# Attention products of one head step on parts of the TensorE array: scores on four 32-column tiles, values on four 32-row tiles

## The chip, the cores and the metric

The kernel runs on one core of a Trainium2 chip. A core has a matrix engine (TensorE, PE in the profile, with its weight loads shown apart as PEld), VectorE (DVE), ScalarE (ACT), GpSimd (POOL) and SyncE (SP), which here issues DMAs. Matrix products read SBUF and write PSUM. The metric is device microseconds of one execution. Six runs of the kernel before gave 1501.7 to 1503.17 us, median 1502.78.

## The reference

The input x has 2048 tokens of 1024 features. It is layer-normalised to xn, and the output is `x + A(xn) + B(xn)`.

A is attention with a small recurrent memory: tokens are cut into 64 segments of 32, each segment is preceded by 8 memory tokens, and 32 heads of 128 features work on these 40 tokens with a causal mask that lets everybody see the memory. The memory rows of a segment's output are the memory of the next segment.

```
for s in range(n_seg):
    h = concatenate([mem, xs])                      # 8 + 32 tokens
    q, k, v = h Wq, h Wk, h Wv                      # 32 heads x 128
    p = softmax(where(mask, q k^T * scale, -1e9))
    o = (p v) Wo
    mem, out_s = o[:8], o[8:]
```

B is a shifted mixer followed by an MLP: `x1 = x + shift(gelu(ln(x) w1)) w2` and `x1 + gelu(ln(x1) w3) w4`, with a hidden width of 3584.

## The kernel before

The program first does B (the mixer with w1 and w2, then the MLP with w3 and w4), and then A. To break the recurrence, A works with an estimate of every segment's memory rows that is computed ahead (tile `MZ`, from mean values), treats the eight memory keys as eight equal entries, and at the end compares the memory that comes out with the estimate. Only if they differ too much would a slow, exact loop at the end of the program run.

A goes through 32 head steps: 4 blocks of 512 tokens (16 segments), and in each block 8 groups of 4 heads. Step i has the block `s.b` and the group `s.hg`. A step has 12 projection chains, counted by c in the loop at lines 897 to 923: c = 0 to 3 are the Q chains of the four heads (`q_chain`, L621), 4 to 7 the K chains (`k_chain`, L637), 8 to 11 the V chains of the four 128-token tiles (`v_chain`, L644). Each is 8 products of 512 columns that accumulate in one PSUM buffer. In the first block each K chain is two runs of 260 columns. The attention products of the step before are hung between the chains: `at(c, f)` calls f after chain c. The order of instructions on each engine is the order of these calls (`manual_schedule`).

For one token tile m of 128 tokens and four heads, `scores` makes per head one product of 128 keys by 132 query columns (four segments of 32 tokens, and one memory column each: W = 33, TW = 132). It lies in the PSUM buffer `psS` (tag A). Of the 128x132 results only the four 32x33 diagonal blocks are wanted, keys of a segment against queries of the same segment. Four exponentials of ScalarE (L671) take these blocks out of `psS` into `ET`. VectorE then transposes in 32x32 blocks (L673), applies the causal mask (L674), sums (L676), takes the reciprocal (L678), normalises (L680) and transposes back (L682). To multiply with the values on the whole array, the probabilities are spread out again into a block-diagonal matrix `BD` of 128x132 per head, with zeros outside the blocks (L686 on VectorE, L688 on POOL for the memory columns). `values` makes one product of 128 keys by 132 columns per head into `psO` (tag B). VectorE adds the estimate `VM` and writes `oX` (L701), and one chain later ScalarE copies the memory columns to `oTs` (L705). POOL also keeps the sums `SSsum` for a check of finiteness and copies the memory scores to `EMs`.

The values of step i come at c = 4, 7, 10 of step i+1 for m = 0, 1, 2 and at c = 1 of step i+2 for m = 3.

PSUM has eight banks: four buffers of one bank with the tag `mm` (`mm_tile`), which all projections and output chains share, and two buffers of two banks, tags A and B (`aux_tile`). A buffer is taken by a new tile when the readers of its last tile are through.

When a block's eight head groups are done, its output projection runs in the second step of the next block (`s.hg == 1`): eight chains of 32 products (`out_chain`, `out_part`, L818), hung at c = 1, each with a load of a piece of `R` (the result of B) that SP issued earlier. For the first block there are also the exact products of the first segment (`first_scores`, `first_soft`, `first_trans`, `first_values`), hung at c = 4, 8, 11 and, a step later, 1. After step 31 a written-out order interleaves the remaining scores and values with the output projection of the last block.

Of the kernel before, what the change touches and what calls it, by code (L numbers as in the profile page):

```python
# [11 lines left out]
DMAX = 1.0e30  # L12

BF16 = mybir.dt.bfloat16
# [7 lines left out]
P = 128  # L22
# [41 lines left out]
def kernel(  # L64
# [69 lines left out]
    def mm_tile(name):  # L134
        return psum.tile([P, 512], F32, tag="mm", bufs=4, name=name)

    def aux_tile(shape, tag, name):
        return psum.tile(shape, F32, tag=tag, bufs=1, name=name)
# [250 lines left out]
    with ExitStack() as p3:  # L389
# [141 lines left out]
        def att_prep():  # L531
            load_xT(0)
            for nm in "qkv":
                need_w(nm, 0)
            need_w("q", 1)
            make_xm(0)
            sm = A["sm"]
            A["BD"] = [sm.tile([P, 4, TW], BF16, name=f"BD{i}") for i in range(3)]
            A["EQ"] = [sm.tile([P, 4, W], F32, name=f"EQ{i}") for i in range(2)]
            for t in A["EQ"]:  # L540
                nc.gpsimd.memset(t[:, :, SEG:W], float(M))
            for nm in ("QZ", "PZ", "VMZ"):
                A[nm] = sm.tile([P, 4, P], BF16, name=nm)
                nc.gpsimd.memset(A[nm][:], 0.0)
            A["VZ"] = sm.tile([P, 512], BF16, name="VZ")
            nc.gpsimd.memset(A["VZ"][:], 0.0)
            A["SS"] = sm.tile([P, 4], F32, name="SSsum")
            nc.gpsimd.memset(A["SS"][:], 0.0)

        for tb in range(4):  # L550
# [29 lines left out]
    specx.close()  # L580

    wpool, xvp, qkv, smp = A["wpool"], A["xvp"], A["qkv"], A["sm"]
    BDs, EQs, SSsum = A["BD"], A["EQ"], A["SS"]
    abig = main.enter_context(tc.tile_pool(name="abig", bufs=1))
    iop = main.enter_context(tc.tile_pool(name="aio", bufs=2))
    oX = abig.tile([P, H, 512], BF16)
# [15 lines left out]
    def new_step(i):  # L602
        s = Step()
        s.i = i
        s.b, s.hg = divmod(i, NHG)
        s.Q = qkv.tile([P, 4, 4 * TW], BF16, tag="Q", bufs=2, name="Q")
        s.K = qkv.tile([P, 4, 512 + M], BF16, tag="K", bufs=2, name="K")
        s.V = qkv.tile([P, 4, 512], BF16, tag="V", bufs=2, name="V")
        if s.hg == 0:
            EMs[s.b] = smp.tile([P, NHG, 4, 4], BF16, tag="EM", bufs=2, name="EM")  # L610
            oTs[s.b] = smp.tile([P, H, 16], BF16, tag="oT", bufs=2, name="oT")
        s.u = [None] * 4
        s.xm = A["m", s.b]
        steps[i] = s
        return s
# [13 lines left out]

    def k_chain(s, hh):  # L630
        w = A["k", s.i]
        n = 2 if s.b == 0 else 1
        c = (512 + M) // 2 if s.b == 0 else 512
        for h2 in range(n):
            ps = mm_tile("psK")
            for k in range(KT):
                nc.tensor.matmul(ps[:, 0:c], w[:, k, hh * P:(hh + 1) * P], s.xm[:, k, h2 * c:(h2 + 1) * c], start=(k == 0), stop=(k == KT - 1))  # L637
            nc.scalar.copy(s.K[:, hh, h2 * c:(h2 + 1) * c], ps[:, 0:c])  # L638

    def v_chain(s, m):  # L640
        w = A["v", s.i]
        ps = mm_tile("psV")
        for k in range(KT):
            nc.tensor.matmul(ps[:], s.xm[:, k, m * P:(m + 1) * P], w[:, k, :], start=(k == 0), stop=(k == KT - 1))  # L644
        nc.scalar.copy(s.V[:, m, :], ps[:])  # L645
# [11 lines left out]
    def mem_cols(s):  # L657
        nc.gpsimd.tensor_copy(s.Q[:].rearrange("p h (s i) -> p h s i", i=W)[:, :, :, SEG], QM[:, hsl(s.hg), 7 + 16 * s.b:23 + 16 * s.b])

    un = [0]  # L660

    def scores(s, m):
        n = un[0]
        un[0] += 1
        ps = aux_tile([P, 4, 256], "A", "psS")
        for hh in range(4):
            nc.tensor.matmul(ps[:, hh, 0:TW], s.K[:, hh, m * P:(m + 1) * P], s.Q[:, hh, m * TW:(m + 1) * TW], start=True, stop=True)  # L667
        ET = smp.tile([P, 4, W], F32, tag="ET", bufs=2, name="ET")
        for j in range(4):
            q = slice(SEG * j, SEG * (j + 1))  # L670
            nc.scalar.activation(ET[q, :, :], ps[q, :, W * j:W * (j + 1)], ACTF.Exp, scale=SCALE)  # L671
        EQ = EQs[n % 2]
        nc.vector.transpose(EQ[:, :, 0:SEG], ET[:, :, 0:SEG])  # L673
        nc.vector.tensor_tensor(EQ[:, :, 0:SEG], EQ[:, :, 0:SEG], causal[:].unsqueeze(1).to_broadcast((P, 4, SEG)), op=ALU.mult)  # L674
        ss = smp.tile([P, 4], F32, tag="ss", bufs=2, name="ss")
        nc.vector.tensor_reduce(ss[:], EQ[:], axis=AX.X, op=ALU.add)  # L676
        rs = smp.tile([P, 4], F32, tag="rs", bufs=2, name="rs")
        nc.vector.reciprocal(rs[:], ss[:])  # L678
        Pn = smp.tile([P, 4, SEG], BF16, tag="Pn", bufs=2, name="Pn")
        nc.vector.tensor_tensor(Pn[:], EQ[:, :, 0:SEG], rs[:].unsqueeze(2).to_broadcast((P, 4, SEG)), op=ALU.mult)  # L680
        PT = smp.tile([P, 4, SEG], BF16, tag="PT", bufs=2, name="PT")
        nc.vector.transpose(PT[:], Pn[:])  # L682
        BD = BDs[n % 3]
        B4 = BD[:].rearrange("p h (j i) -> p h j i", i=W)
        so = segone[:].unsqueeze(1).to_broadcast((P, 4, 4))
        nc.vector.tensor_tensor(B4[:, :, :, 0:SEG], PT[:].unsqueeze(2).to_broadcast((P, 4, 4, SEG)),  # L686
                                so.unsqueeze(3).to_broadcast((P, 4, 4, SEG)), op=ALU.mult)
        nc.gpsimd.tensor_tensor(B4[:, :, :, SEG], ET[:, :, SEG:W].to_broadcast((P, 4, 4)), so, op=ALU.mult)  # L688
        nc.gpsimd.tensor_tensor(SSsum[:], SSsum[:], ss[:], op=ALU.add)
        nc.gpsimd.tensor_copy(EMs[s.b][:, s.hg, :, m:m + 1], ET[:, :, SEG:W])  # L690
        s.u[m] = BD

    def values(s, m):
        BD = s.u[m]
        ps = aux_tile([P, 4, 256], "B", "psO")
        for hh in range(4):
            nc.tensor.matmul(ps[:, hh, 0:TW], s.V[:, m, hh * P:(hh + 1) * P], BD[:, hh, :], start=True, stop=True)  # L697
        p4 = ps[:, :, 0:TW].rearrange("p h (j i) -> p h j i", i=W)
        j0 = 1 if (s.b == 0 and m == 0) else 0
        z = 7 + 16 * s.b + 4 * m  # L700
        nc.vector.tensor_tensor(  # L701
            oX[:, hsl(s.hg), m * P:(m + 1) * P].rearrange("p h (j i) -> p h j i", i=SEG)[:, :, j0:4, :],
            p4[:, :, j0:4, 0:SEG],
            VM[:, hsl(s.hg), z + j0:z + 4].unsqueeze(3).to_broadcast((P, 4, 4 - j0, SEG)), op=ALU.add)
        return lambda: nc.scalar.copy(oTs[s.b][:, hsl(s.hg), 4 * m:4 * m + 4], p4[:, :, :, SEG])  # L705

    QZ, PZ, VMZ, VZ = A["QZ"], A["PZ"], A["VMZ"], A["VZ"]

# [83 lines left out]
        total(d, 0, M)  # L792

    def finite():
        cnt = smp.tile([P, 5], F32, tag="cnt", name="cnt")
        nc.vector.tensor_scalar(cnt[:, 0:4], SSsum[:], DMAX, None, op0=ALU.is_le)
        nc.vector.tensor_reduce(cnt[:, 4:5], cnt[:, 0:4], axis=AX.X, op=ALU.add)
        nc.vector.tensor_scalar(chk[:, 2 * NV:2 * NV + 1], cnt[:, 4:5], -1.0, 4.0, op0=ALU.mult, op1=ALU.add)

    Rts = {}  # L800

# [47 lines left out]
    for i in range(NS):  # L849
# [7 lines left out]
        def at(c, f, *a):  # L857
            hooks.setdefault(c, []).append((f, a))

        def at_values(c, u, m):  # L860
            later = []
            at(c, lambda: later.append(values(u, m)))
            at(c + 1, lambda: later.pop()())

        if pp is not None:
            at_values(1, pp, 3)
        if p is not None:
            at(0, scores, p, 0)
            for m in range(3):
                at(3 * m + 3, scores, p, m + 1)  # L870
                at_values(3 * m + 4, p, m)
        if 4 < s.hg and s.b + 1 < NB:
            for k in range(3 * s.hg - 15, min(3 * s.hg - 12, KT)):
                at(2 + 4 * (k % 3), make_xm, s.b + 1, (k,))
# [5 lines left out]
            at(1, first_values, pp)  # L880
        if s.hg == 1 and s.b > 0:
            for c in range(8):
                at(1, out_chain, s.b - 1, c)
        if s.hg == 2 and s.b > 0:
            at(2, norm_sums, s.b - 1)
            for j in range(4):
# [37 lines left out]
        if last:  # L924
            b = s.b
            load_Rt(b, 0)
            load_Rt(b, 1)
            hp = H - 4
            scores(s, 0)
            out_part(b, 0, 0, hp)  # L930
            values(p, 3)()
            scores(s, 1)
            out_part(b, 1, 0, hp)
            values(s, 0)()
            scores(s, 2)
            out_part(b, 2, 0, hp)
            values(s, 1)()
            scores(s, 3)
            out_part(b, 0, hp, H)
            out_part(b, 1, hp, H)  # L940
            out_part(b, 3, 0, hp)
            values(s, 2)()
            out_part(b, 2, hp, H)
            out_part(b, 3, hp, H)
            values(s, 3)()
            norm_sums(b)
            for j in range(4):
                norm_recip(b, j)
            norm_apply(b)
            norm_add(b)  # L950
            compare(b)
            finite()
            out_chain(b, 4)
            out_chain(b, 5)
            out_chain(b, 6)
            verdict()
            out_part(b, 7, 0, H, 2)
# [129 lines left out]
```

## Time and profile before

| | |
|---|---|
| median of six runs | 1502.78 us |
| the profiled execution | 1502.8 us |
| its span, first to last instruction | 1501.0 us |
| granted TensorE clock | 1.000 |
| instructions | 23719 |
| matrix products / weight loads | 9330 / 9456 records |
| score products (L667) | 512 of 128x132, 221 ns each |
| value products (L697) | 512 of 128x132, 221 ns each |
| exponentials (L671) | 512 of 32x132, 271 ns each |
| VectorE spreading into `BD` (L686) | 128, 703 ns each |
| VectorE adding into `oX` (L701) | 120 of 128x512, 683 ns each, and 8 shorter |

A line of a group names the source line, the engine, the operation, the tiles (written, then read), and for TensorE the part of the array that is used as rows*columns ahead of the shape of the moving operand; then the count, the busy time in us, the mean duration of one in ns, and the idle time of the engine just before. Products are pipelined: the next one starts long before the last has left the array, so a duration of 221 ns is not the time that one more product costs. Their busy time is the union of the durations. The timeline has the start in us, the time until the last one of the row ends, the engine, line and tiles, and the count of instructions merged in the row.

### The profile page before, as it was taken

The page shows a single profiled execution, that of the slowest core. Times are in us where ns is not written, and L with a number is a line of the kernel's source. Part 1 is how long each engine was busy: PE and PEld are TensorE (multiplying, and loading weights), DVE is VectorE, ACT ScalarE, POOL GpSimd, SP SyncE. Part 2 cuts the span into 40 slices and gives each one's busy share as a digit, 9 for nine tenths or more (in the row PEclk, how much of TensorE's full clock was granted, in tenths as well). Part 3 has the DMA queues.
Part 4 walks back from the last instruction along what each step waited for, and adds up shares of the span by engine and source line. Part 5 has one row for each costly group of instructions (what it writes and reads, how often), then busy time and mean ns, then how long its engine had stood idle before and what let it go on. Part 6 is the DMA issues. An engine that isn't in the chain of part 4 may idle for free.

```text
span 1501.0 us, 23719 instructions
## 1 busy us (share of the span) xinstructions
PE 1486.1 (99%) x9330; PEld 784.9 (52%) x9456; DVE 666.5 (44%) x1561; ACT 467.5 (31%) x1247; POOL 257.2 (17%) x707
## 2 busy tenths in 40 slices
PE   9999999999999999999999999999999999999998
PEld 7844444444444466666644544444544544444544
DVE  8283010010110226666622777731676650576654
ACT  5633202103012035454501444420434430244420
POOL 6152131211110202121210111110111110111110
PEclk9999999999999999999999999999999999999999
DMA  8599753553121545474522454431455441344302
GB/s 216 138 283 214 264 189 99 184 174 133 63 92 40 199 136 188 143 223 141 183 71 64 139 166 141 154 102 50 140 153 156 141 133 58 105 138 140 117 0 72
DMA packets 189172, 208.11 MB, mean 139 GB/s; under 512 B 50168, under 2 KB 157832, under 8 KB 189056
## 3 DMA queue, kind: packets, MB, share of 16 engines
q1 hardware_dynamic: 180768, 178.82, 39.6%
q0 software_dynamic: 8288, 27.72, 5.3%
q8 instruction: 76, 1.25, 0.4%
q14 instruction: 40, 0.33, 0.1%
HBM read 170.07 MB, written 25.17 MB: 130 GB/s over the span
## 4 chain that ended last, share of the span: by engine, by line
PE 98%; DMA 1%; issue 0%; SPq 0%; DVE 0%
PE psK L637 15%; PE psP L818 15%; PE psQ L621 15%; PE psV L644 15%; PE ps L555 13%; PE ps L573 13%; PE ps L366 4%; PE ps L265 3%; PE psO L697 2%; PE psS L667 2%; PE psM L653 1%; DMA w_sb<-in_B_w_dram 1%; PE psvb L425 1%; PE psG L446 1%; PE ps L294 0%
## 5 line engine op out<-in xcount | busy, mean ns | idle before, releaser
L818 PE MATMUL psP<-wo_sb,oX 128*128 128x512 bf16 (+1 forms) x1036 | 221.7, 372 | 1.1
L671 ACT ACTIVATE ET<-psS 32x132 f32<-32x132 f32 x512 | 139.0, 271 | 203.7 <-PE psS L667 198.1
L573 PE MATMUL ps<-w,hT_all 128*128 128x512 bf16 x874 | 193.7, 379 | 1.2
L637 PE MATMUL psK<-xT,w 128*128 128x512 bf16 x747 | 176.3, 379 | 1.1
L621 PE MATMUL psQ<-xT,w 128*128 128x512 bf16 x750 | 175.8, 379 | 1.1
L644 PE MATMUL psV<-w,xT 128*128 128x512 bf16 x745 | 175.0, 379 | 1.0
L818 PEld LDWEIGHTS <-oX 128*128 128x128 bf16 x1056 | 102.9, 98 | 115.7
L637 PEld LDWEIGHTS <-w 128*128 128x128 bf16 x1280 | 121.3, 98 | 80.1
L556 ACT ACTIVATE hT_all<-ps 128x512 bf16<-128x512 f32 x112 | 66.8, 597 | 283.5 <-PE ps L555 283.5
L621 PEld LDWEIGHTS <-w 128*128 128x128 bf16 x1024 | 96.8, 98 | 104.1
L573 PEld LDWEIGHTS <-hT_all 128*128 128x128 bf16 x896 | 87.1, 98 | 103.8
L688 POOL TENSOR_TENSOR BD<-ET,c_segone_sb 128x16 bf16<-128x16 f32 x128 | 33.7, 263 | 491.5 <-ACT ET L671 491.5
L628 DVE TENSOR_TENSOR Q<-psQ,QM 128x512 bf16<-128x512 f32 (+1 forms) x128 | 85.6, 679 | 60.9 <-ACT Q L627 39.8
L644 PEld LDWEIGHTS <-xT 128*128 128x128 bf16 x768 | 72.1, 98 | 73.5
L673 DVE STREAM_TRANSPOSE EQ<-ET 128x128 f32<-128x128 f32 x128 | 39.8, 311 | 157.0 <-ACT ET L671 156.8
L645 ACT CAST V<-psV 128x512 bf16<-128x512 f32 x128 | 75.0, 586 | 110.1 <-PE psV L644 100.1
L638 ACT CAST K<-psK 128x512 bf16<-128x512 f32 (+1 forms) x160 | 80.4, 502 | 90.8 <-PE psK L637 89.0
L555 PE MATMUL ps<-xn3T,w3a 128*128 128x512 bf16 x448 | 97.7, 379 | 0.0
L555 PE MATMUL ps<-xn3T,w3b 128*128 128x512 bf16 x448 | 97.7, 379 | 0.0
L824 DVE TENSOR_TENSOR ot<-psP,Rt 128x512 bf16<-128x512 f32 (+1 forms) x33 | 22.2, 675 | 157.3 <-PE psP L818 157.3
L686 DVE TENSOR_TENSOR BD<-PT,c_segone_sb 128x512 bf16<-128x512 bf16 x128 | 90.0, 703 | 4.5
L701 DVE TENSOR_TENSOR oX<-psO,VM 128x512 bf16<-128x512 f32 (+1 forms) x128 | 86.3, 674 | 7.8 <-PE psO L697 7.8
(157 smaller groups left out, 1499.8 us busy)
## 6 DMA issues: line engine op xcount, KB each, us to landing
w<-in_A_Wq_dram SPq DMA_DIRECT2D x32, 1024.0 KB, 5.4
w<-in_A_Wk_dram SPq DMA_DIRECT2D x32, 1024.0 KB, 5.4
w<-in_A_Wv_dram SPq DMA_DIRECT2D x32, 1024.0 KB, 5.4
R_scratch<-x POOLq DMA_DIRECT2D x16, 512.0 KB, 7.2
R<-R_scratch SPq DMA_DIRECT2D x16, 512.0 KB, 7.1
chunk<-in_A_Wv_dram SPq DMA_DIRECT2D x8, 1024.0 KB, 5.4
R_scratch<-R POOLq DMA_DIRECT2D x16, 512.0 KB, 4.1
chunk<-in_A_Wo_dram SPq DMA_DIRECT2D x8, 1024.0 KB, 5.8
```

Source lines behind the costliest of these rows:

```text
L555: nc.tensor.matmul(ps[:], w3[:, k, (f % FH) * P:(f % FH + 1) * P], xn3Ts[tb][:, :, k, :], start=(k == 0), stop=(k == KT - 1))
L573: nc.tensor.matmul(ps[:], h3T[:, f, j * P:(j + 1) * P], w4t[f // 4][:, f % 4, ch * 512:(ch + 1) * 512], start=(f == 0), stop=(f == FT - 1))
L621: nc.tensor.matmul(ps[:], w[:, k, hh * P:(hh + 1) * P], s.xm[:, k, 0:512], start=(k == 0), stop=(k == KT - 1))
L628: nc.vector.tensor_tensor(q3[:, j0:16, 0:SEG], p3_[:, j0:16, :], QM[:, 4 * s.hg + hh, z + j0:z + 16].unsqueeze(2).to_broadcast((P, 16 - j0 ...
L637: nc.tensor.matmul(ps[:, 0:c], w[:, k, hh * P:(hh + 1) * P], s.xm[:, k, h2 * c:(h2 + 1) * c], start=(k == 0), stop=(k == KT - 1))
L638: nc.scalar.copy(s.K[:, hh, h2 * c:(h2 + 1) * c], ps[:, 0:c])
L644: nc.tensor.matmul(ps[:], s.xm[:, k, m * P:(m + 1) * P], w[:, k, :], start=(k == 0), stop=(k == KT - 1))
L645: nc.scalar.copy(s.V[:, m, :], ps[:])
L671: nc.scalar.activation(ET[q, :, :], ps[q, :, W * j:W * (j + 1)], ACTF.Exp, scale=SCALE)
L686: nc.vector.tensor_tensor(B4[:, :, :, 0:SEG], PT[:].unsqueeze(2).to_broadcast((P, 4, 4, SEG)), so.unsqueeze(3).to_broadcast((P, 4, 4, SEG) ...
L701: nc.vector.tensor_tensor(oX[:, hsl(s.hg), m * P:(m + 1) * P].rearrange("p h (j i) -> p h j i", i=SEG)[:, :, j0:4, :], p4[:, :, j0:4, 0:SE ...
L818: nc.tensor.matmul(ps[:, 0:w], oX[:, h, m * P:(m + 1) * P], wo_sb[:, h, cc], start=(h == 0), stop=(h == H - 1))
```

## The change

Scores and values of a step are each done for all four heads and all four token tiles at once, 16 items (m, head), on parts of the array.

`scores` makes for each item and each segment j a product of that segment's 32 keys by its own 33 query columns. The 32 keys are the weights; the output goes to the 32 PSUM partitions of segment j, so that the four segments use four 32-column tiles of the array. 64 products fill two `mm` buffers, and two exponentials read them whole.

`soft` runs the same VectorE sequence as before, once for the 16 items (512 columns instead of four times 128). There is no block-diagonal spreading, except for the last item.

`values` makes for 15 of the items and each segment j a product with the segment's 32 rows of V and of the probabilities: 60 products on four 32-row tiles, into four banks (one for each j) of the tags A and B. Fifteen items of 33 columns are what fits into a bank; the sixteenth is one ordinary product of 128 rows by 132 columns with a `BD` of its own, into an `mm` buffer `psE`. VectorE adds into `oX` with nine instructions, and `mem_values` copies the memory columns with seven ScalarE instructions.

All of it is hung at c = 7: the scores of step i-1, then the values of step i-2, then the softmax of step i-1; `mem_values` follows at c = 10. The output chains of a finished block move from c = 1 to c = 9. K and V tiles are taken at their first chain instead of at the step's start. The end of the program is put into a new order.

```diff
-    def scores(s, m):
-        ps = aux_tile([P, 4, 256], "A", "psS")
-        for hh in range(4):
-            nc.tensor.matmul(ps[:, hh, 0:TW], s.K[:, hh, m * P:(m + 1) * P], s.Q[:, hh, m * TW:(m + 1) * TW], start=True, stop=True)
-        for j in range(4):
-            nc.scalar.activation(ET[q, :, :], ps[q, :, W * j:W * (j + 1)], ACTF.Exp, scale=SCALE)
...
+    def scores(s):
+        s.ps = [mm_tile("psS") for _ in range(2)]
+        s.ET = smp.tile([P, 16, W], F32, tag="ET", name="ET")
+        for g in range(2):
+            for it in range(8):
+                m, hh = divmod(8 * g + it, 4)
+                for j in range(4):
+                    k0 = m * P + SEG * j
+                    nc.tensor.matmul(s.ps[g][SEG * j:SEG * (j + 1), it * W:(it + 1) * W], s.K[:, hh, k0:k0 + SEG],
+                                     s.Q[:, hh, (4 * m + j) * W:(4 * m + j + 1) * W], start=True, stop=True)
+            nc.scalar.activation(s.ET[:, 8 * g:8 * g + 8, :], s.ps[g][:, 0:8 * W].rearrange("p (t i) -> p t i", i=W), ACTF.Exp, scale=SCALE)
+
+    def soft(s):
+        nc.vector.transpose(EQ[:, :, 0:SEG], ET[:, :, 0:SEG])
...
+        nc.vector.transpose(s.PT[:, :, 0:SEG], Pn[:])
+        nc.gpsimd.tensor_copy(s.PT[:, :, SEG:W], ET[:, :, SEG:W])
...
+    def values(s):
+        s.O = [aux_tile([P, 2, 512], t, "psO") for t in "AB"]
+        s.E = mm_tile("psE")
+        for it in range(15):
+            for j in range(4):
+                m, hh = divmod(it, 4)
+                q = slice(SEG * j, SEG * (j + 1))
+                nc.tensor.matmul(s.O[j // 2][:, j % 2, it * W:(it + 1) * W], s.V[q, m, hh * P:(hh + 1) * P], s.PT[q, it, 0:W], start=True, stop=True)
+        nc.tensor.matmul(s.E[:, 0:TW], s.V[:, 3, 3 * P:4 * P], s.BD[:], start=True, stop=True)
...
-        if pp is not None:
-            at_values(1, pp, 3)
         if p is not None:
-            at(0, scores, p, 0)
-            for m in range(3):
-                at(3 * m + 3, scores, p, m + 1)
-                at_values(3 * m + 4, p, m)
+            at(7, scores, p)
+        if pp is not None:
+            at(7, values, pp)
+            at(10, mem_values, pp)
+        if p is not None:
+            at(7, soft, p)
...
-                at(1, out_chain, s.b - 1, c)
+                at(9, out_chain, s.b - 1, c)
...
-            scores(s, 0)
+            scores(s)
+            values(p)
+            soft(s)
             out_part(b, 0, 0, hp)
-            values(p, 3)()
-            scores(s, 1)
+            mem_values(p)
             out_part(b, 1, 0, hp)
-            values(s, 0)()
-            scores(s, 2)
+            values(s)
             out_part(b, 2, 0, hp)
-            values(s, 1)()
-            scores(s, 3)
+            mem_values(s)
             out_part(b, 0, hp, H)
             out_part(b, 1, hp, H)
-            out_part(b, 3, 0, hp)
-            values(s, 2)()
             out_part(b, 2, hp, H)
-            out_part(b, 3, hp, H)
-            values(s, 3)()
+            out_chain(b, 3)
             norm_sums(b)
```

More of the change, by code (lines that the diff above doesn't have):

```diff
@@ L537, in att_prep @@
             sm = A["sm"]
[L538 to L541, printed above, removed]
+            A["EQ"] = sm.tile([P, 16, W], F32, name="EQ")
+            nc.gpsimd.memset(A["EQ"][:, :, SEG:W], float(M))
             for nm in ("QZ", "PZ", "VMZ"):
@@ L546, in att_prep @@
             nc.gpsimd.memset(A["VZ"][:], 0.0)
-            A["SS"] = sm.tile([P, 4], F32, name="SSsum")
+            A["SS"] = sm.tile([P, 16], F32, name="SSsum")
             nc.gpsimd.memset(A["SS"][:], 0.0)
@@ L582 @@
     wpool, xvp, qkv, smp = A["wpool"], A["xvp"], A["qkv"], A["sm"]
-    BDs, EQs, SSsum = A["BD"], A["EQ"], A["SS"]
+    EQ, SSsum = A["EQ"], A["SS"]
     abig = main.enter_context(tc.tile_pool(name="abig", bufs=1))
@@ L606, in new_step @@
         s.Q = qkv.tile([P, 4, 4 * TW], BF16, tag="Q", bufs=2, name="Q")
-        s.K = qkv.tile([P, 4, 512 + M], BF16, tag="K", bufs=2, name="K")
-        s.V = qkv.tile([P, 4, 512], BF16, tag="V", bufs=2, name="V")
         if s.hg == 0:
@@ L611, in new_step @@
             oTs[s.b] = smp.tile([P, H, 16], BF16, tag="oT", bufs=2, name="oT")
-        s.u = [None] * 4
         s.xm = A["m", s.b]
@@ L631, in k_chain @@
         w = A["k", s.i]
+        if hh == 0:
+            s.K = qkv.tile([P, 4, 512 + M], BF16, tag="K", bufs=2, name="K")
         n = 2 if s.b == 0 else 1
@@ L641, in v_chain @@
         w = A["v", s.i]
+        if m == 0:
+            s.V = qkv.tile([P, 4, 512], BF16, tag="V", bufs=2, name="V")
         ps = mm_tile("psV")
@@ L658, in mem_cols @@
         nc.gpsimd.tensor_copy(s.Q[:].rearrange("p h (s i) -> p h s i", i=W)[:, :, :, SEG], QM[:, hsl(s.hg), 7 + 16 * s.b:23 + 16 * s.b])
-    un = [0]
-    def scores(s, m):
-        n = un[0]
-        un[0] += 1
-        ps = aux_tile([P, 4, 256], "A", "psS")
-        for hh in range(4):
-            nc.tensor.matmul(ps[:, hh, 0:TW], s.K[:, hh, m * P:(m + 1) * P], s.Q[:, hh, m * TW:(m + 1) * TW], start=True, stop=True)
-        ET = smp.tile([P, 4, W], F32, tag="ET", bufs=2, name="ET")
-        for j in range(4):
-            q = slice(SEG * j, SEG * (j + 1))
-            nc.scalar.activation(ET[q, :, :], ps[q, :, W * j:W * (j + 1)], ACTF.Exp, scale=SCALE)
[L672 to L705, printed above, removed]
+    def scores(s):
[9 more added lines that the diff above has]
+            nc.scalar.activation(s.ET[:, 8 * g:8 * g + 8, :], s.ps[g][:, 0:8 * W].rearrange("p (t i) -> p t i", i=W), ACTF.Exp, scale=SCALE)
@@ new lines, in soft @@
+    def soft(s):
+        ET = s.ET
+        nc.vector.transpose(EQ[:, :, 0:SEG], ET[:, :, 0:SEG])
+        nc.vector.tensor_tensor(EQ[:, :, 0:SEG], EQ[:, :, 0:SEG], causal[:].unsqueeze(1).to_broadcast((P, 16, SEG)), op=ALU.mult)
+        ss = smp.tile([P, 16], F32, tag="ss", name="ss")
+        nc.vector.tensor_reduce(ss[:], EQ[:], axis=AX.X, op=ALU.add)
+        rs = smp.tile([P, 16], F32, tag="rs", name="rs")
+        nc.vector.reciprocal(rs[:], ss[:])
+        Pn = smp.tile([P, 16, SEG], BF16, tag="Pn", name="Pn")
+        nc.vector.tensor_tensor(Pn[:], EQ[:, :, 0:SEG], rs[:].unsqueeze(2).to_broadcast((P, 16, SEG)), op=ALU.mult)
+        s.PT = smp.tile([P, 16, W + 1], BF16, tag="PT", name="PT")
+        nc.vector.transpose(s.PT[:, :, 0:SEG], Pn[:])
+        nc.gpsimd.tensor_copy(s.PT[:, :, SEG:W], ET[:, :, SEG:W])
+        s.BD = smp.tile([P, TW], BF16, tag="BD", name="BD")
+        nc.gpsimd.tensor_tensor(s.BD[:].rearrange("p (j i) -> p j i", i=W), s.PT[:, 15, 0:W].unsqueeze(1).to_broadcast((P, 4, W)),
+                                segone[:].unsqueeze(2).to_broadcast((P, 4, W)), op=ALU.mult)
+        nc.gpsimd.tensor_tensor(SSsum[:], SSsum[:], ss[:], op=ALU.add)
+        nc.gpsimd.tensor_copy(EMs[s.b][:, s.hg, :, :].rearrange("p h m -> p m h"), ET[:].rearrange("p (m h) i -> p m h i", h=4)[:, :, :, SEG])
@@ new lines, in values @@
+    def values(s):
[7 more added lines that the diff above has]
+        nc.tensor.matmul(s.E[:, 0:TW], s.V[:, 3, 3 * P:4 * P], s.BD[:], start=True, stop=True)
+        z = 7 + 16 * s.b
+        h0 = 4 * s.hg
+        e3 = s.E[:, 0:TW].rearrange("p (j i) -> p j i", i=W)
+        nc.vector.tensor_tensor(oX[:, h0 + 3, 3 * P:4 * P].rearrange("p (j i) -> p j i", i=SEG), e3[:, :, 0:SEG],
+                                VM[:, h0 + 3, z + 12:z + 16].unsqueeze(2).to_broadcast((P, 4, SEG)), op=ALU.add)
+        for j in range(4):
+            o4 = s.O[j // 2][:, j % 2, 0:15 * W].rearrange("p (t i) -> p t i", i=W)
+            for m0, m1, hn in ((1 if s.b == 0 and j == 0 else 0, 3, 4), (3, 4, 3)):
+                n = (m1 - m0) * hn
+                nc.vector.tensor_tensor(
+                    oX[:, h0:h0 + hn, :].rearrange("p h (m c) -> p m h c", c=P)[:, m0:m1, :, SEG * j:SEG * (j + 1)],
+                    o4[:, 4 * m0:4 * m0 + n, 0:SEG].rearrange("p (m h) i -> p m h i", h=hn),
+                    VM[:, h0:h0 + hn, z:z + 16].rearrange("p h (m j) -> p m h j", j=4)[:, m0:m1, :, j].unsqueeze(3).to_broadcast((P, m1 - m0, hn, SEG)), op=ALU.add)
@@ new lines, in mem_values @@
+    def mem_values(s):
+        h0 = 4 * s.hg
+        oT = oTs[s.b]
+        e3 = s.E[:, 0:TW].rearrange("p (j i) -> p j i", i=W)
+        nc.scalar.copy(oT[:, h0 + 3, 12:16], e3[:, :, SEG])
+        for r in range(2):
+            o4 = s.O[r][:, :, 0:15 * W].rearrange("p j (t i) -> p j t i", i=W)[:, :, :, SEG]
+            for j in range(2):
+                nc.scalar.copy(oT[:, h0:h0 + 4, :].rearrange("p h (m j) -> p m h j", j=4)[:, 0:3, :, 2 * r + j], o4[:, j, 0:12].rearrange("p (m h) -> p m h", h=4))
+            nc.scalar.copy(oT[:, h0:h0 + 3, 12 + 2 * r:14 + 2 * r].rearrange("p h j -> p j h"), o4[:, :, 12:15])
@@ L794, in finite @@
     def finite():
[L795 to L798, printed above, removed]
+        cnt = smp.tile([P, 17], F32, tag="cnt", name="cnt")
+        nc.vector.tensor_scalar(cnt[:, 0:16], SSsum[:], DMAX, None, op0=ALU.is_le)
+        nc.vector.tensor_reduce(cnt[:, 16:17], cnt[:, 0:16], axis=AX.X, op=ALU.add)
+        nc.vector.tensor_scalar(chk[:, 2 * NV:2 * NV + 1], cnt[:, 16:17], -1.0, 16.0, op0=ALU.mult, op1=ALU.add)
     Rts = {}
@@ L858, in at @@
             hooks.setdefault(c, []).append((f, a))
[L860 to L863, printed above, removed]
+        if p is not None:
+            at(7, scores, p)
         if pp is not None:
-            at_values(1, pp, 3)
+            at(7, values, pp)
+            at(10, mem_values, pp)
         if p is not None:
-            at(0, scores, p, 0)
-            for m in range(3):
-                at(3 * m + 3, scores, p, m + 1)
-                at_values(3 * m + 4, p, m)
+            at(7, soft, p)
         if 4 < s.hg and s.b + 1 < NB:
```

## The prediction

> **What bounds the kernel now.** I read five views: busy time by engine, the chain that ended last, the groups by form, and the timeline at two places.
>
> ```profile
> PE 1486.1 (99%) x9330; PEld 784.9 (52%) x9456; DVE 666.5 (44%) x1561; ACT 467.5 (31%) x1247; POOL 257.2 (17%) x707
> ...
> PE 98%; DMA 1%; issue 0%; SPq 0%; DVE 0%
> ```
>
> TensorE is the chain from end to end; no other engine sets the time. So the change is worth what it does to TensorE's time. VectorE's 44% and ScalarE's 31% matter only if they make TensorE wait. In the chain in order of time, one head step looks like this:
>
> ```profile
> 1204.01 0.23 PE psS L667 x4
> ...
> 1205.97 0.23 PE psO L697 x4
> 1206.20 3.45 PE psQ L621 x16
> ```
>
> Four score products take 0.23 us, then the projections go on at once. The groups, each shape apart (count | busy us, mean ns of one | idle before):
>
> ```profile
> L697 PE MATMUL psO<-BD,V 128*128 128x132 bf16 x512 | 50.9, 221 | 0.1
> L667 PE MATMUL psS<-Q,K 128*128 128x132 bf16 x512 | 50.4, 221 | 0.0
> L425 PE MATMUL psvb<-xb,chunk 128*128 128x63 bf16 x256 | 9.0, 193 | 0.0
> L260 PE MATMUL psX<-c_segone_sb,x 128*128 128x4 bf16 x128 | 4.3, 164 | 0.0
> L725 PE MATMUL psZ<-KZ,QZ 128*128 128x40 bf16 x32 | 2.1, 180 | 0.0
> ```
>
> Matmuls overlap, so the pace (start to start of two load-and-multiply pairs) has to be worked out: a run of n lasts one duration plus n-1 paces. psS: 128 runs of 4 in 50.4 us are 394 ns each, (394-221)/3 = 57.6 ns for 132 columns. psvb: 8 runs of 32, (1125-193)/31 = 30 ns for 63 columns. psZ: 8 runs of 4, about 27 ns for 40. psX: 8 runs of 16, (537-164)/15 = 25 ns for 4 columns. Below some 50 columns a pair costs about 25 ns however short it is. Two places already use a part of the array, 8 rows (L400) and one column (L835, L837):
>
> ```profile
> 125.50 1.03 PE L366 MATMUL ps<-w_sb,hT_all 128*128 128x512 bf16 x4
> 126.46 0.35 PE L400 MATMUL ps<-c_eye_sb,m 8*128 8x9 bf16 x8
> 126.74 1.04 PE L555 MATMUL ps<-xn3T,w3a 128*128 128x512 bf16 x4
> ```
>
> ```profile
> 1488.21 0.81 PE L818 MATMUL psP<-wo_sb,oX 128*128 128x512 bf16 x3
> 1488.95 0.08 PEld L835 LDWEIGHTS <-c_qones_sb 128*1 128x1 bf16 x1 [0.42 <-issue]
> 1488.95 0.22 PE L835 MATMUL psC<-chk,c_qones_sb 128*1 128x141 bf16 x1
> 1488.95 0.21 PEld L837 LDWEIGHTS <-c_qones_sb 128*1 128x1 bf16 x3
> 1489.01 0.35 PE L837 MATMUL psC<-chk,c_qones_sb 128*1 128x141 bf16 x3
> ...
> 1489.29 0.77 PEld L818 LDWEIGHTS <-oX 128*128 128x128 bf16 x8
> ```
>
> The 8-row run: (350-162)/7 = 27 ns a pair, the floor again. Switching costs: the last 512-column product before L400 starts at 125.50+1.03-0.38 = 126.15, so the next was due 0.216 us later at 126.37; it starts at 126.46, 0.09 us late. Leaving is 0.07 us late. Around the one-column run both are 0.09 us late. So a change of shape costs about 93 ns.
>
> **The change, part by part.** Own time of the profiled execution: 1502.8 us, span 1501.0 with 1.8 around it, at the median of the runs (1502.78).
>
> Removed from TensorE: per head step 16 score and 16 value pairs of 132 columns, eight runs of 0.231 us (4 x 57.6), 1.85 us; 32 steps make 59.2 us. Even free products could save no more.
>
> Added: per step 64 score pairs (32 columns of weights, 33 streamed) and 60 value pairs (32 rows, 33 streamed), 124 pairs, plus one ordinary pair of 57.6 ns for the sixteenth item. No row shows 33 columns on four different tiles. From below: if the tiles fully overlap, four pairs share one 25 ns slot, 6.25 ns. From above: psvb's pace is 30 ns and the one-column pairs' is 61 ns for 141 columns; a weight load that no longer hides under so short a product could add some 15 ns, so 40 ns. I take 25 ns: 33 columns lie between psX's 4 and psZ's 40, and the only row with a narrow row tile, L400, stands there too. 32 x 124 x 25 ns = 99.2 us; the ordinary pair 1.8 us.
>
> Shape changes: full to column tiles, to row tiles, to full, three a step: 32 x 3 x 93 ns = 8.9 us, where before there were none (a product after a run of psS starts 58 ns on, a plain pace). Bounds: nothing if the loads run ahead, 12 us if each were 0.12.
>
> PSUM: the mm ring has four buffers. psE holds one from c=7 until its ScalarE copy at c=10. In steps with the first segment's work (7 of them hold psE as well), psVZ and psZ take two more after the first value projection, so the next projection waits for the 586 ns V copy with only 4 x 56 + 4 x 25 = 320 ns of products as cover: 0.3 us, 2.1 us in all (0 to 4). Elsewhere a projection of 1.73 us covers the copy in the three buffers left; so it does for the eight output chains now at c=9.
>
> VectorE: four softmax and expansion rounds of 3.05 us a step (311+292+291+178+292+311+703+674 ns) become one of about 3.7 and nine adds of about 3.5 us (384-element adds 544 ns in L701's short form): 12.2 to 7.2 us. ScalarE: sixteen exponentials of 271 ns become two of about 0.39 (L267's 256 columns), four copies of 173 ns become seven. POOL's small work shrinks. None is gained, because TensorE's "idle before" psS and psO is 0.0 and 0.1 us. It does not hurt either: work bunched at c=7 ends about 10.6 us later, the first Q projection that needs VectorE ends at 3.4 + 5 x 1.73 = 12.0 us, and behind it three more buffers are free. If this cover went, each us late would be a us a step, 32 us. The output chains need the adds only at heads 28 to 31, 6 us in. At the end, values wait for softmax (11 us) behind 12 us of output products. No DMA is added; SP's and POOL's queues keep their loads. Moving the output chains from c=1 to c=9 puts their R loads in SP's queue behind the k and v weight loads (5.4 us each); the third chain is the first to need one, 13.8 us later.
>
> Sum: -59.2 + 99.2 + 1.8 + 8.9 + 2.1 = +52.8 us, to 1555.6.
>
> A rule on it: the Trainium skill, "TensorEngine Tiling (Array Packing)", Instruction Overhead, gives each matmul about 60 cycles whatever its free size below 60, and warns against taking the tiling factor from a dimension already small. This change takes it from 132 columns to 33; by that rule each pair stays at the 25 ns measured. Against it, "TensorE: Matmul & The Clock Gate", Part 3, has tiles of one pack start some 4 ns apart; an estimate of 8 ns for load and product gives 31.7 us instead of 99.2, and 1488. No run shown here has such a pack.
>
> **The rivals.**
>
> *The tiles overlap* (other side). Four neighbours write separate partitions or banks, and use different weights. For it: at 1488.95 two weight loads and a product start within one hundredth of a microsecond, so the front end can start instructions far quicker than every 25 ns. Against: no two products in the trace start closer than 25 ns. At 6.25 ns: 24.8 + 12.8 - 59.2 = -21.6, 1481. It decides below (59.2-12.8)/(32 x 124) = 11.7 ns a pair; between 6 and 11 lies 1481 to 1500. Instruction fetch sets a limit near that: 76 packets of the instruction queue took 0.4% of 16 x 1501 us, 1.3 us for 16 KB; 248 short instructions are nearly one packet in 1 us.
>
> *Half overlap*: only one product, or loads limiting at 12 to 20 ns. Score pairs at 6.25 and value pairs at 25: 32 x (64 x 6.25 + 60 x 25) = 60.8, +14.4, 1517.
>
> *Dearer pairs*: the 32-column loads don't hide. At 33 ns +84.6 (1587), at 40 +112 (1615). For it: load and product now last about equally long. Against: in the one-column run the next load starts under the running product.
>
> **How the numbers follow.** Serial at the floor, 22 to 30 ns: 0.42, 1544 to 1575, my forecast 1555.6. Half overlap: 0.16, 1503 to 1544. Full overlap: 0.30, 1480 to 1501. Dearer: 0.12, above 1575. Faster is the full overlap without its edge, 0.28; same (within 0.2%, 3 us, about what a measurement tells from no change) 0.04 at 11 to 12.5 ns; slower 0.68. The range is 1480 to 1592: it leaves out the dearest pairs (0.08) and a little below.
>
> **What would show it.** psS and psO runs: 64 and 60 pairs at 25 ns, so 1.6 and 1.5 us of chain each step, then 1.73 us projections untouched; starts 0.09 us late at three places a step; VectorE busy near 500 us and TensorE still at 98% or more. Wrong if neighbouring starts of different tiles stand closer than 12 ns, if weight loads rather than products set the pace, or if TensorE waits for PSUM in most steps.

## The result, and the profile after

The changed kernel takes 1498.77 us (median of 18 runs, 1497.81 to 1500.97) against 1502.49 us before: ratio 0.9976, 95% interval 0.9969 to 0.9982. It is 3.7 us faster, where 52.8 us slower was forecast. The profiled execution has a span of 1497.4 us, 3.6 less than before.

Busy time by engine and the head of the chain that ended last, after:

```profile
PE 1472.1 (98%) x12314; PEld 760.2 (51%) x12432; DVE 500.7 (33%) x1017; ACT 347.1 (23%) x895; POOL 196.8 (13%) x450
...
PE 95%; DVE 3%; issue 1%; DMA 1%; SPq 0%; ACT 0%; POOL 0%; DVEq 0%; POOLq 0%; ACTq 0%
```

TensorE's busy time fell by 14.0 us although it runs some 3000 products more. The span fell only by 3.6 us: TensorE is now idle for 25.3 us of it, before for 14.9, and VectorE has a place of 3% in the chain, where it had none. So there are two questions: why did the products become cheaper, and where did the rest of the gain go?

The groups by form, after (count | busy us, mean ns of one | idle before):

```profile
L667 PE MATMUL psS<-Q,K 128*32 128x33 bf16 x2048 | 21.7, 182 | 0.0
L697 PE MATMUL psO<-PT,V 32*128 32x33 bf16 x1920 | 20.0, 177 | 0.0
```

and a step of a later block in the chain in order of time:

```profile
1172.73 0.61 PE psS L667 x64
1173.34 0.56 PE psO L697 x60
1173.90 0.16 PE psE L698
```

All attention products of a step, their changes of shape included, take 1.33 us. Before it was eight runs of 0.23, 1.85 us. Of the 0.61 us, some 0.10 is the change of shape behind it, so 64 pairs take 0.51 us, 8 ns a pair; the value pairs come to 7.5 ns. In the trace the starts lie in groups of four, 3 to 4 ns apart, and each group begins some 25 ns after the start of the one before it. So the four tiles do work at the same time, and the 25 ns that the trace of before showed for every short pair is what one tile needs, not what the engine needs. This regular picture holds for the first 32 pairs after a change of shape (6.3 ns a pair); the later ones follow evenly at 8.3 ns.

The length of a step is the time from its first Q product to that of the next step. Before, a step of block 0 and one of block 3 in the chain in order of time:

```profile
654.34 0.21 PE psQ L621
...
679.75 0.22 PE psQ L621
...
1202.29 1.73 PE psQ L621 x8
...
1224.86 1.73 PE psQ L621 x8
```

and after:

```profile
658.31 0.22 PE psQ L616
...
684.78 0.22 PE psQ L616
...
1203.02 4.10 PE psQ L616 x19
...
1225.07 4.10 PE psQ L616 x19
```

A steady step of blocks 1 to 3 takes 22.05 us after and 22.57 to 22.58 before: 0.525 us gained. Times 32 this is 16.8 us. But in block 0 such a step takes 26.46 us after and 25.41 before: 1.05 us lost. What TensorE waited for, the four longest in total (us, times, longest):

```profile
PE psV L643 <- DVE eZ L744: 6.0, 7, 0.9
PE psV L643 <- ACT V L644: 2.5, 7, 0.4
PE psE L698 <- issue: 1.9, 1, 1.9
PE psT L252 <- DVE xn L229: 1.8, 2, 1.0
```

Before, only its waits in the first 15 us stood there. Seven steps of block 0 have two waits each. The timeline of one shows how they come about (start, time to the end of the last one, in brackets the idle time before):

```profile
673.99 2.47 DVE L708 TENSOR_TENSOR oX<-psO,VM 128x256 bf16<-128x256 f32 x8
...
675.53 0.26 PE L742 MATMUL psZ<-KZ,QZ 128*128 128x40 bf16 x4
...
676.14 3.61 PE L643 MATMUL psV<-w,xm 128*128 128x512 bf16 x16 [0.36 <-ACT V L644]
...
679.66 0.71 DVE L682 STREAM_TRANSPOSE PT<-Pn 128x512 bf16<-128x512 bf16 x1
680.29 0.27 DVE L744 SCALAR_TENSOR_TENSOR eZ<-psZ,c_mask_sb 40x160 f32<-40x160 f32 x1
...
680.62 1.89 PE L643 MATMUL psV<-w,xm 128*128 128x512 bf16 x8 [0.86 <-DVE eZ L744]
```

psZ, the first segment's scores, is complete at 675.8, but VectorE still has the adds of the values and then the whole softmax of 16 items in its queue. It reads psZ at 680.29. Until then psZ holds one of the four `mm` buffers, psE holds another, and the V chains wait: once for the V copy and once for psZ. Measured start to start the two cost 0.51 and 1.07 us, 1.58 a step, 11.0 us in seven steps. The third wait, 1.9 us once in step 3, has no releaser in the profile.

In sum: -16.8 + 11.0 + 1.9 = -3.9 us; the measured spans differ by -3.6.

### The profile page after: what moved, and what is told of

It reads as the page before. It is cut to its first block, busy times and chain, and to the rows that moved or that the text cites. A ratio compares the mean times of both kernels' runs of the same rounds, so it can differ in the third digit from the quotient of the medians.

```text
span 1497.4 us, 28216 instructions
## 1 busy us (share of the span) xinstructions
PE 1472.1 (98%) x12314; PEld 760.2 (51%) x12432; DVE 500.7 (33%) x1017; ACT 347.1 (23%) x895; POOL 196.8 (13%) x450
## 4 chain that ended last, share of the span: by engine, by line
PE 95%; DVE 3%; issue 1%; DMA 1%; SPq 0%; ACT 0%; POOL 0%; DVEq 0%; POOLq 0%; ACTq 0%
PE psK L634 15%; PE psP L835 15%; PE psQ L616 15%; PE ps L553 13%; PE ps L571 13%; PE psV L643 12%; PE ps L366 4%; PE ps L265 3%; PE psS L667 1%; PE psO L697 1%; PE psM L652 1%; DVE oX L708 1%; DMA w_sb<-in_B_w_dram 1%; PE psvb L425 1%; PE psG L446 1%
## 5 line engine op out<-in xcount | busy, mean ns | idle before, releaser
L634 PEld LDWEIGHTS <-w 128*128 128x128 bf16 x1280 | 125.1, 98 | 99.1
L643 PE MATMUL psV<-w,xT 128*128 128x512 bf16 x744 | 169.2, 379 | 2.5 <-DVE eZ L744 0.9
L616 PE MATMUL psQ<-xT,w 128*128 128x512 bf16 x744 | 169.1, 379 | 1.3
L634 PE MATMUL psK<-xT,w 128*128 128x512 bf16 x763 | 169.4, 379 | 0.3
L616 PEld LDWEIGHTS <-w 128*128 128x128 bf16 x1024 | 98.8, 98 | 115.9
L702 DVE TENSOR_TENSOR oX<-psE,VM 128x128 bf16<-128x128 f32 x32 | 9.3, 292 | 217.9 <-PE psE L698 217.9
L708 DVE TENSOR_TENSOR oX<-psO,VM 128x96 bf16<-128x96 f32 (+2 forms) x256 | 82.1, 393 | 0.0
L553 PEld LDWEIGHTS <-w3b 128*128 128x128 bf16 x448 | 43.5, 98 | 52.0
L553 PEld LDWEIGHTS <-w3a 128*128 128x128 bf16 x448 | 43.5, 98 | 51.7
L481 DVE TENSOR_SCALAR xt<-xt,lnst 128x1024 bf16<-128x1024 bf16 x16 | 8.7, 546 | 180.6 <-POOL R L480 180.6
```

What stands on the lines that cost most here:

```text
L553: nc.tensor.matmul(ps[:], w3[:, k, (f % FH) * P:(f % FH + 1) * P], xn3Ts[tb][:, :, k, :], start=(k == 0), stop=(k == KT - 1))
L616: nc.tensor.matmul(ps[:], w[:, k, hh * P:(hh + 1) * P], s.xm[:, k, 0:512], start=(k == 0), stop=(k == KT - 1))
L708: nc.vector.tensor_tensor(oX[:, h0:h0 + hn, :].rearrange("p h (m c) -> p m h c", c=P)[:, m0:m1, :, SEG * j:SEG * (j + 1)], o4[:, 4 * m0:4 ...
```

## The experiments

Every ratio is to the kernel before, run on the same chip; in parentheses stands its 95% interval. The edits are against the changed kernel, and dots mark lines left out.

**Pairs of one tile in a row.** Is it the change of tile that makes the pairs cheap?

```diff
-            for it in range(8):
+            for it, j in [(it, j) for j in range(4) for it in range(8)]:
...
-        for it in range(15):
-            for j in range(4):
+        for it, j in [(it, j) for j in range(4) for it in range(15)]:
```

> Same products as the changed kernel, but all items of segment 0 first, then segment 1 and so on, so that 8 score pairs and 15 value pairs in a row go to the same tile. Theory (pairs on different tiles overlap, a tile by itself takes a new pair only every 25 ns): the pace of psS and psO goes from 8 ns to about 25 ns, 124 x 17 ns = 2.1 us a step, 32 steps +67 us, about 1566 us. Rival (a narrow pair is cheap in itself, whatever tile the one before it was on): pace still 8 ns, about 1499 us.

1539.69 us, ratio 1.0248 (1.0232 to 1.0264), 41 us above the changed kernel. The same products in the chain of a steady step:

```profile
1174.19 1.15 PE psS L666 x64
1175.33 1.36 PE psO L695 x60
```

Less the 0.10 us for the change of shape behind each, this is 16 and 21 ns a pair. Within a tile the trace has start after start 25 or 26 ns apart; around the seam from one tile to the next the spacings alternate (3, 23, 2, 23 ns), as they would if pairs of both ran at once, and the mean stays below 25. Direction and floor are as the theory has it, the rise of 67 us was too high because it left out these seams. A narrow pair is not cheap in itself.

**Two tiles alternating.**

```diff
-            for it in range(8):
+            for it, j in [(it, j) for h in (0, 2) for it in range(8) for j in (h, h + 1)]:
...
-        for it in range(15):
-            for j in range(4):
+        for it, j in [(it, j) for h in (0, 2) for it in range(15) for j in (h, h + 1)]:
```

> Same products, alternating between segments 0 and 1 and then between 2 and 3. Theory (each tile takes a pair every 25 ns, and 8 ns is the pace at which pairs are handed out): two tiles give 12.5 ns a pair, 124 x 4.5 ns x 32 = +18 us, about 1517 us. Rival (any change of tile is enough, the pace is that of the handing out): 8 ns, about 1499 us.

1508.27 us, ratio 1.0042 (1.0029 to 1.0055), 9.5 us above the changed kernel. Score and value pairs take 9.7 and 11.3 ns in the mean; in the regular stretches two starts lie 2 to 5 ns apart and the next two 25 ns on, 12.5 ns a pair. Again the seam between the halves saves something. With one, two and four tiles the pace in the regular stretches is 25, 12.5 and 6.3 ns: a tile takes one pair every 25 ns. In these kernels each tile also has its own place in PSUM (32 partitions for the scores, a bank for the values); no run tells a limit of the tile from one of that place.

**More changes of shape.** Scores and values in halves, interleaved.

```diff
-            at(7, scores, p)
+            at(7, scores, p, (0,))
...
-            at(7, values, pp)
+            at(7, values, pp, range(8))
...
+            at(7, scores, p, (1,))
...
+            at(7, values, pp, range(8, 15))
```

> The changed kernel with scores and values cut in halves and interleaved (scores 0, values 0, scores 1, values 1): five changes of the array's shape a step instead of three, the same pairs. Theory (a change of shape costs about 0.1 us each time, as L400 and the one-column run showed): 2 x 0.1 us x 31 steps = +6 us, about 1505 us. Rival (the changes run under the pairs): no difference, 1499 us.

1500.29 us, ratio 0.9988 (0.9978 to 0.9997): 1.5 us above the changed kernel, not 6. A steady step:

```profile
1173.06 0.31 PE psS L668 x32
1173.37 0.30 PE psO L699 x32
1173.68 0.31 PE psS L668 x32
1173.99 0.28 PE psO L699 x28
1174.27 0.16 PE psE L702
```

1.36 us instead of 1.33. Each change does cost its time (start to start 110 ns from scores to values and 102 back, of which some 6 are the pairs' own pace), but the pairs now run at 6.6 ns in the mean instead of 8.0 and 7.5, because each run ends before the slower stretch begins. Both theories were half right. Why the first 32 pairs run at 6.3 ns and the later ones at 8.3 was not tried; the supply of instructions is one candidate.

**The first segment's work ahead of the bundle.**

```diff
-            at(4, first_scores, p)
-            at(8, first_soft, p)
+            at(2, first_scores, p)
+            at(5, first_soft, p)
```

> The changed kernel with the first segment's exact products earlier in the step: first_scores after chain 2 instead of 4, first_soft after chain 5 instead of 8, so ahead of the bundle at chain 7. Theory (the gain is given back in the first block, where psVZ and psZ come right behind the bundle, find three PSUM buffers, and VectorE reads psZ only after 7 us of queued work): 7 steps x 1.58 us = 11 us gone, about 1488 us. Rival (the first block has to wait for that work wherever it is put): the stalls move to the K chains and the time stays near 1499 us.

1486.76 us, ratio 0.9898 (0.9883 to 0.9914), 12.0 us below the changed kernel. All that TensorE still waited for:

```profile
PE psW L197 <- DVE fill L176: 1.5, 1, 1.5
PE psO L697 <- issue: 1.4, 1, 1.4
PE psT L252 <- DVE xn L229: 1.2, 2, 0.8
PE ps L280 <- ACT xn2T L255: 0.2, 1, 0.2
```

Both waits of the V chains are gone, and they did not move to the K chains: steps of block 0 now take 24.89 us, 0.52 less than in the kernel before, as everywhere else. So the missing gain had been given back in block 0.

**psE copied at once.** Which of the two is the root, the held buffer or VectorE's queue?

```diff
     def values(s):
         ...
+        nc.scalar.copy(oTs[s.b][:, h0 + 3, 12:16], e3[:, :, SEG])
...
     def mem_values(s):
...
-        nc.scalar.copy(oT[:, h0 + 3, 12:16], e3[:, :, SEG])
```

> The changed kernel with the ScalarE copy out of psE right behind the values at chain 7 instead of chain 10, so that the fourth PSUM buffer is free again when the V chains need it. Theory A (the buffer held by psE is the root of both waits of a first-block step): 11 us gone, about 1488 us. Theory B (VectorE's queue is the root of the second): only the wait for the V copy goes, 7 x 0.51 us = 3.6 us, about 1495 us.

1495.23 us, ratio 0.9948 (0.9934 to 0.9961), 3.5 us below the changed kernel, the figure of theory B. The waits, of which three are shown, tell more than either theory said:

```profile
PE psZT L755 <- DVE PZ L750: 5.6, 7, 1.7
PE psT L252 <- DVE xn L229: 2.1, 2, 1.3
PE psE L698 <- issue: 1.5, 1, 1.5
```

With a fourth buffer the V chains wait for nothing. But the first segment's softmax is as late as ever on VectorE, and three chains later the transposes that need it (psZT) wait instead. The buffer decided where the lateness is felt, VectorE's queue how large it is.

**Softmax at chain 10.**

```diff
-            at(7, soft, p)
+            at(10, soft, p)
```

> The changed kernel with the softmax hung at chain 10 instead of 7, behind first_soft. In a first-block step VectorE then reads psZ after the nine adds, not after another 3.9 us of softmax. Theory B (VectorE's queue is the root of the second wait): the second wait of 1.07 us goes, 7 x 1.07 = 7.5 us, about 1491 us, the first of 0.51 us stays. Theory A (the buffer held by psE is the root): the second wait shrinks little, about 1498 us.

1491.46 us, ratio 0.9929 (0.9915 to 0.9942), 7.3 us below the changed kernel, as theory B has it.

```profile
PE psV L643 <- ACT V L644: 2.1, 6, 0.4
PE psE L698 <- issue: 1.7, 1, 1.7
```

The wait for eZ is gone, the one for the V copy stays (six times instead of seven).

**Both.** The early first segment with psE copied at once.

```diff
-            at(4, first_scores, p)
-            at(8, first_soft, p)
+            at(2, first_scores, p)
+            at(5, first_soft, p)
...
+        nc.scalar.copy(oTs[s.b][:, h0 + 3, 12:16], e3[:, :, SEG])
```

> First segment's products early and psE freed at once, together. Theory: the waits of the first block are gone by either of the two, so this adds nothing to the better one: about 1487.5 us, -15 us against the kernel before; per step 22.05 us in blocks 1 to 3 and 24.9 us in block 0. Rival: the two remove different waits and add up, about 1484 us.

1487.82 us, ratio 0.9904 (0.9889 to 0.9919): nothing on top of the early first segment, as the theory said. The steps take 22.05 and 24.89 us.

**The wait without a releaser.** In every version whose pairs run fast, one wait of 1.4 to 1.9 us stands in step 3, in the value pairs or at psE. The instruction queue of the profile moved 99 packets of 16 KB in the changed kernel and 76 before. The change adds 2976 weight loads and as many products, so 23 packets more carry 5952 instructions more, 259 each; an estimate from this is blocks of 256 instructions of 64 bytes. One step's attention has 248. A packet takes 1.0 to 1.1 us, and in step 3 one starts 0.5 us after the first score pair. The next two kernels have the early first segment and shift all later instructions, the first by 32 pairs, the second by 12:

```diff
         def warm(c):
             ...
+                for i in range(32):
+                    nc.tensor.matmul(ps[:, 0:8], fill[:, 0:P], fill[:, 0:8], start=True, stop=True)
```

> The kernel with the first segment's products early, and 32 short pairs (64 TensorE instructions) more at the start, where TensorE waits for the first input anyway, so that all later instructions lie 64 places further on in the instruction stream. Theory (the single wait of 1.4 to 1.9 us in the value pairs of step 3, for which the profile names no releaser, is TensorE running out of fetched instructions: 248 instructions in 1.1 us against a fetch of 16 KB, and in that step a fetch starts within 0.1 to 0.6 us of the first score pair): the wait is gone from step 3 or is found in another step, and the time is up to 1.5 us less, about 1485.5 us. Rival (something of step 3 itself holds the pair): the same wait in the same step, 1487 us.

> As the run with 64 instructions more, with 12 short pairs (24 instructions). Theory (instruction fetch): the wait of step 3 changes its length or place with the shift, by about the 24 instructions. Rival: the same wait of 1.4 us at the same pair.

> The kernel with the first segment's products early once more, beside the two shifted ones on one chip: about 1487 us, and the wait in the value pairs of step 3 at the same pair as before under both theories.

1489.09, 1487.19 and 1487.10 us; ratios 0.9909 (0.9893 to 0.9926), 0.9900 (0.9883 to 0.9917) and 0.9899 (0.9883 to 0.9916). Waits of the kernel shifted by 64 instructions:

```profile
PE psO L699 <- issue: 1.4, 1, 1.4
PE psV L645 <- issue: 0.8, 1, 0.8
```

of the one shifted by 24:

```profile
PE psO L699 <- issue: 1.0, 1, 1.0
PE psV L645 <- issue: 0.7, 1, 0.7
```

and of the one not shifted:

```profile
PE psO L697 <- issue: 1.5, 1, 1.5
```

With 64 the wait left step 3 (24.89 us like its neighbours) and two others appeared, at 643.5 us in step 4 and at 691.9 us in step 6. With 24 it stayed in step 3, shortened from 1.5 to 1.0 us, and another came in step 6. Unshifted it was where it had been. So the place in the instruction stream makes this wait, and nothing in step 3 does.

A count in the traces says which place. In the six traces of experiments that have all products on record, counted from the start, 8897 TensorE instructions (loads, products and those of its sequencer) lie ahead of the instruction that waits in step 3: the same number in the four kernels that are not shifted, whose products come in three different orders, and in the one shifted by 24, where the wait moved from the 53rd value pair to the 41st, 24 instructions back in the work. Ahead of the later waits lie 9665, and in both shifted kernels 10945, which is 3 x 256 and 8 x 256 more. And in all versions such a wait ends 2.3 to 2.7 us after a packet of the instruction queue began. So it stands at the end of a block of 256 instructions, as the fetch theory says. Why just these blocks come late, and most others do not, is open.

The hoped-for 1.5 us were not to be had by these shifts: one wait goes and others come. In two profiled executions (the softmax at chain 10, and the shift by 64) the granted TensorE clock was also 0.5 for 3.4 us, from less than 1 us behind such a wait; 512-column products start 427 ns apart there instead of 216. With the wait of 1.4 us and this stretch, step 6 of the kernel shifted by 64 takes 28.13 us, 3.24 more than steps without. The longest wait, 1.9 us in the changed kernel, has no such stretch behind it. The other executions of the kernel shifted by 64 had a mean clock of 1.0 and took as long, so this does not explain its 2 us over the unshifted one.

The best version is the one with the first segment early: 1486.76 and 1487.10 us in two comparisons, 1.0% below the kernel before and 0.8% below the changed one.

## Why the prediction was wrong

**The direction was wrong, and the step that failed is "I take 25 ns" for a pair on four different tiles.** The sum's 99.2 us for 124 pairs measured 32 x 0.96 = 31 us. The row it leaned on, L400, has eight pairs on one and the same row tile; its pace is real (25 ns start to start in the trace, 27 by the prediction's working), and the run with one tile at a time shows it again. It was read as the pace of the engine, while it was the pace of a tile. No row of the trace before had two tiles side by side, and the two bounds were 6.25 and 40 ns; the measured 8 lies near the lower one. What spoke for it was in the same fence: at 1488.95 two loads and a product started within a hundredth of a microsecond.

The two rules of the Trainium skill now sort themselves. "TensorE: Matmul & The Clock Gate", Part 3, has tiles of a pack start some 4 ns apart: measured, 3 to 4 ns. The prediction's estimate from it, 8 ns a pair, was the measured mean. "TensorEngine Tiling (Array Packing)", Instruction Overhead, holds for each tile by itself: 25 ns at 33 columns, but four such at once.

**The rest of the sum, term by term.** The removed products were 59.7 us (59.2 predicted), the ordinary pair 2.2 (1.8). The three changes of shape cost 93, 103 and 104 ns, 9.6 us (8.9): this term, taken from two places of the trace before, held. The wait for the V copy was foreseen in its place, steps and cause, and measured 3.6 us (2.1). VectorE fell to 500.7 us as forecast.

**"It does not hurt either", of VectorE's bunched work, failed in block 0.** The cover was worked out for the Q chains of an ordinary step, and there it held: steps of blocks 1 to 3 lose nothing. What was overlooked is a reader queued between: `first_soft` at chain 8, whose scores lie in PSUM from 675.8 to 680.29 us while VectorE works off its queue. That is 7.5 us in seven steps. Nor was the wait at a block of instructions (1.9 us) in the sum; instruction fetch appeared only under the overlap rival, as a limit.

**The rivals.** Full overlap was the right mechanism. By its own formula 8 ns give 31.7 + 12.8 - 59.2 = -14.7 us; the 11 us beyond the terms foreseen (1.5 more for the V copy, 7.5 for psZ, 1.9 in step 3) turned it into -3.7. So the measured time lies in this rival's range of 1480 to 1501 us, but near its upper end and because of waits that the rival did not have. The point from which it decides, 11.7 ns, holds for the terms that were in the sum: two tiles, at 9.7 and 11.3 ns a pair, come out 0.4% (some 6 us) slower than before, but with those 11 us of waits in them; without these they would be some 5 us faster. Nothing of dearer pairs was seen: loads of 32 columns keep up at 8 ns a pair.

## What to carry to other kernels

A pace read from a run on one part of the array says nothing about runs on different parts; if no row shows the case, the lower bound deserves as much weight as the nearest row. Products on several tiles have to be issued in turn, neighbours on different tiles, else most of the gain is lost. And when work is bunched, look on each engine for everything that is queued behind the bunch, in the rare steps too: here seven steps of thirty-two gave back two thirds of the gain, and moving one piece of work ahead of the bundle recovered it.

## What was not expected of the hardware

- Pairs on different tiles overlap even with the weights loaded anew for each: one pair per tile every 25 ns, 6.3 ns a pair on four tiles for the first 32 pairs after a change of shape, 8.3 ns after that. Why it slows was not settled.
- Pairs of two tiles run at once even where the program has all pairs of the one before those of the other, around the seam.
- Single waits of 0.7 to 1.9 us in or right behind short pairs, which move when 24 or 64 instructions are put in far ahead of them: where they could be counted, they stand at ends of blocks of 256 instructions, and all end 2.3 to 2.7 us after a packet of the instruction queue began.
- The granted clock at 0.5 for 3.4 us behind two of these waits (1.4 and 1.7 us) and not behind the others; why was not tried.
